# A fourth raw-weight buffer, one buffer fewer for a tanh, and q/k rows that are no longer loaded

## The chip, the cores and the metric

The kernel runs on one core of one Trainium2 chip. The metric is the device time of one execution in microseconds. The kernel before took 527.47 us, the median of three runs (524.8 to 528.14).

## What is computed

A gated linear attention is followed by two feed-forward layers. The reference walks through 768 positions of 16 (batch, head) pairs; the kernel computes the same in chunks of 128 positions.

```python
for t in range(S):
    m_new = np.maximum(f_gate[:, :, t] + m, i_gate[:, :, t])
    f_stab = np.exp(f_gate[:, :, t] + m - m_new)
    i_stab = np.exp(i_gate[:, :, t] - m_new)
    C = f_stab * C + i_stab * outer(vt, kt)
    n = f_stab * n + i_stab * kt
    y[:, :, t] = sigmoid(o_gate[t]) * (C @ qt) / max(abs(n . qt), 1)
# layer one: 1536 tokens x 320, hidden width 1536
xn = x / sqrt(mean(x * x) + 1e-6) * rms_g
x = (silu(xn @ w_gate) * (xn @ w_val)) @ w_out
# layer two
out = (sigmoid(x @ w_gate2) * (x @ w_val2)) @ w_out2
```

All inputs and the output are float32. The sizes are B, H, S, D = 2, 8, 768, 40.

## The kernel before

The work has three parts that overlap. The attention works on 12 units, one for each chunk of 128 positions and batch (`unit`, u = 0 to 11). A unit loads q and k in a layout of 104 partitions (`qk`: four heads on rows 0 to 39, four on rows 64 to 103, rows 40 to 63 zero), its natural rows `nat` and the transposed q `qt`, forms decay factors `E` with an exponential on ACT (L313 or L307), scores on PE (L323), weighs them on DVE (L330), and multiplies with v on PE (L343). The scores read rows 0 to 39 and 64 to 103 of `qk` alone (L322). Two units make one token group of 256 tokens.

Layer one runs over six token groups and 12 blocks of 128 hidden units (`up1`, `act1`, `dn1`): 16 matmuls of 256 columns into one PSUM bank `up` (L460), a tanh on ACT (L489), two products on DVE (L490, L491), a split of the result into two float32r parts (L492, L493), and six matmuls into the accumulators (L471 to L473). Layer two does the same with its own weights. Its token groups are of 256, 512, 512 and 256 tokens (`G2`). For groups of 512 the gate goes to a bank `up` and the value to a bank `sc`, the tanh (L544) writes a tile `th2` in SBUF, L545 multiplies in it, L546 and L547 read it.

The float32 weights are split into two float32r parts on the chip. A layer has 12 blocks, each in two pieces of 128 x 544 words, so 24 pieces a layer; here they are numbered 0 to 47, and block m of layer one has pieces 2m and 2m+1. A piece goes through these steps, each an instruction of 0.7 us or so:

- load (L98, issued by SyncE) into a buffer `wraw`, of which there are three
- L102 (`w_pre`, ACT) reads it and writes `wT`, of which there are also three
- L109 (`w_low`, ACT) rewrites the low half of `wraw` in place; it needs nothing but the landed words
- L113 (`w_bits`, DVE) joins both into `wT`; it is the last reader of `wraw`
- L122 (`w_hi`, ACT) writes the high part `wH`
- L126 (`w_lo`, DVE) writes the low part `wL`, and `wT` is free

The 24 pieces of layer one are made while the first token group goes through the layer, up to 96 us. The pieces of layer two are made from 238 us on, while groups 4 and 5 of layer one and group 0 of layer two take turns on PE, block by block, up to 341 us; a block's weights go where layer one's block of one before lay, so they follow its last use.

Each engine executes in order. Up to the first two units the order is written out; after that a scheduler sets it from priorities (`want` with times from the table `T`), from dependencies and from free buffers in its own model of time. SyncE issues nearly all loads, in order, so a load that waits for its buffer holds up the loads behind it.

Of the kernel before, what the change touches and what calls it, by code (L numbers as in the profile page):

```python
# [7 lines left out]
F32 = mybir.dt.float32  # L8
F32R = mybir.dt.float32r
BF16 = mybir.dt.bfloat16  # L10
I32 = mybir.dt.int32
# [6 lines left out]
B, H, S, D = 2, 8, 768, 40  # L18
# [17 lines left out]
WP = WC // 2  # L36
# [22 lines left out]
def attention_then_two_moe(tc, fi, fir, qk, qt3, nat, w1, w2, rms_g, consts, out):  # L59
    nc = tc.nc  # L60
# [5 lines left out]
    mp = ctx.enter_context(tc.tile_pool(name="mp", bufs=2))  # L66
# [27 lines left out]
    wH, wL, wraw, wT = {}, {}, {}, {}  # L94

    def w_load(moe, m, p):
        t = wraw[moe, m, p] = mp.tile([128, WP, 2], I32, tag="wraw", name="wraw", bufs=3)
        nc.sync.dma_start(out=t, in_=w64[moe][m, :, p * WP:(p + 1) * WP, :])  # L98

    def w_pre(moe, m, p):  # L100
# [141 lines left out]
    def a_load(u, parts=(0, 1, 2, 3)):  # L242
        d = X.setdefault(u, {})
        if 0 in parts:
            d["qk"] = ap.tile([QR, 2, 4, L], F32, tag="qk", name="qk")
            nc.sync.dma_start(out=d["qk"], in_=qk[u])
        if 1 in parts:
            d["nat"] = ap.tile([128, NAT], F32, tag="nat", name="nat")
            nc.sync.dma_start(out=d["nat"][:, 9 * D:], in_=nat[u, :, 9 * D:])
        if 3 in parts:  # L250
            nc.sync.dma_start(out=d["nat"][:, 0:9 * D], in_=nat[u, :, 0:9 * D])
        if u >= B and 2 in parts:
            d["qt"] = ap.tile([KR, NG, L], F32, tag="qt", name="qt")
            nc.sync.dma_start(out=d["qt"], in_=qt3[u])
# [254 lines left out]
    p2 = [None]  # L509
# [27 lines left out]
    def act2(g, m, gt, vl):  # L537
        if G2[g][1] == 2:
            th = mp.tile([128, 256], F32, tag="th", name="th")
            hT = hts[1, g, m] = mp.tile([128, 2, 256], F32R, tag="hT", name="hT", bufs=3)  # L540
        else:
            th = p2[0].tile([128, 512], F32, tag="th2", name="th2")
            hT = hts[1, g, m] = p2[0].tile([128, 2, 512], F32R, tag="hT2", name="hT2", bufs=3)
        nc.scalar.activation(th, gt, AF.Tanh, scale=0.5)  # L544
        nc.vector.scalar_tensor_tensor(out=th, in0=th, scalar=1.0, in1=vl, op0=ALU.add, op1=ALU.mult)  # L545
        nc.scalar.copy(hT[:, 0, :], th)  # L546
        nc.vector.tensor_tensor(out=hT[:, 1, :], in0=th, in1=hT[:, 0, :].bitcast(F32), op=ALU.subtract)  # L547
# [54 lines left out]
    def w_step(k):  # L602
        moe, m, p = piece(k)
        if k < 3:
            return
        t = t_slot(first(moe, None, m)) + T["w1" if moe else "w0"] + p
        if k > 3:
            want(t - T["wld"], lambda: w_load(moe, m, p))
        want(t - 3, lambda: w_pre(moe, m, p))
        want(t - 2, lambda: w_bits(moe, m, p))  # L610
        want(t - 1, lambda: w_hi(moe, m, p))
        want(t, lambda: w_lo(moe, m, p))

    def unit(u):
        t = t_unit(u) + (u % B) * T["skew"]
        st = [
            [a_scale, a_bcast_pe, a_exp] if u > B else [a_scale, a_exp],
            [a_scores, a_wv, a_gate],
            [a_weigh] if u < PE_ADD else [a_weigh, a_state],
            [a_out, a_decay, a_state, a_update] if u < PE_ADD else [a_out, a_decay, a_update],  # L620
            [a_norm1, a_norm1b, a_norm1c],
            [a_norm2],
            [a_norm3, a_flip],
            [a_xt],
        ]
        if u >= B:
            want(t - T["uld"], lambda: a_load(u))
        for k, fns in enumerate(st):
            want(t + k * T["stg"], *[lambda fn=fn: fn(u) for fn in fns])
# [7 lines left out]
    with tc.manual_schedule(engines=set(engines)):  # L637
        nc.vector.memset(junk, 0.0)
        nc.sync.dma_start(out=fi0, in_=fi[:, :, 0:L])
        nc.scalar.dma_start(out=fiS, in_=fi[:, :, L:])  # L640
        a_load(0, (0,))
        w_load(0, 0, 0)
        nc.scalar.copy(tiny, junk[:, 0:1])
        for t, fill in ((ident, 1.0), (identb, 1.0)):
# [33 lines left out]
        g_max()  # L678
        w_pre(0, 0, 0)
        w_load(0, 0, 1)  # L680
        a_load(1, (0,))
        a_load(0, (1,))
        g_move()
# [92 lines left out]
    for s, (moe, g, m, f, l) in enumerate(steps):  # L776
        if s == 0:
            att_ctx.close()
            p2[0] = ctx.enter_context(tc.tile_pool(name="p2", bufs=2))
        if s == NI:  # L780
            for k in range(2 * NM, 2 * NM + 2):
                w_step(k)
        r = []
        want(t_slot(s), lambda: in_order(lambda: r.append((up1, up2)[moe](g, m))))
        want(t_slot(s) + 1, lambda: (act1, act2)[moe](g, m, *r[0]))
        if s > 1:
            dn(s - 2)
            x2_ready(s - 2)
            if steps[s - 2][0:2] == (0, 5) and steps[s - 2][2] < NM - 1:
                for k in range(2):  # L790
                    w_step(2 * NM + 2 * (steps[s - 2][2] + 1) + k)
# [73 lines left out]
```

## Time and profile before

| | |
|---|---|
| median of three runs | 527.47 us |
| lowest, highest | 524.8, 528.14 us |
| the profiled execution, device time | 524.49 us |
| its span, first to last instruction | 522.7 us |
| PE busy | 503.7 us |
| DVE, ACT, POOL busy | 260.4, 232.0, 105.3 us |
| moved by DMA | 43.09 MB |

The profile is of one execution, and its rows are in microseconds from the start of its span. Busy PE means that a matmul is under way, not that PE is at its peak, since matmuls are pipelined. A row of the list of waits says which engine stood idle before which instruction, what ended the wait, and the total, the number of times and the longest.

### The profile page before, as it was taken

To read this page: it belongs to the slowest core of one execution; us is meant where nothing else is said; L and a number is where in the kernel's file an instruction comes from. 1 tells how busy PE (TensorE), PEld (TensorE's weight loads), DVE (VectorE), ACT (ScalarE), POOL (GpSimd) and SP (SyncE) were. 2 spreads that over 40 slices of the span, in tenths; PEclk is the share of its full clock that TensorE was granted. 3 is DMA by queue.
4 is the path that set the end of the run, shared out by engine and by line. 5 is a ranking of instruction groups with operands and counts; after the bars stand their busy time and mean duration, and the time that the engine had idled before them with its cause. 6 is when DMAs were issued, how large, how long until landed. Compare 5 with 4: busy or idle time off the path is not lost.

```text
span 522.7 us, 9043 instructions
## 1 busy us (share of the span) xinstructions
PE 503.7 (96%) x3576; PEld 466.8 (89%) x3576; DVE 260.4 (50%) x540; ACT 232.0 (44%) x518; POOL 105.3 (20%) x164
## 2 busy tenths in 40 slices
PE   7889899999999999999999899999999999999996
PEld 5668799999999999999999899998888888888996
DVE  5668789744255445557665646533233233222332
ACT  4667889733233333326576657442222222221322
POOL 7013135443243243232221211110000000000000
PEclk9769979999999999999999999999999999999999
DMA  6588787711041030102153242000000010000100
GB/s 193 182 255 298 246 262 231 240 55 41 1 112 44 25 114 16 41 2 85 35 198 113 92 165 87 1 1 25 1 1 2 0 51 0 1 0 1 51 1 26
DMA packets 15752, 43.09 MB, mean 82 GB/s; under 512 B 1822, under 2 KB 6734, under 8 KB 15710
## 3 DMA queue, kind: packets, MB, share of 16 engines
q1 hardware_dynamic: 15518, 42.27, 25.4%
q8 instruction: 28, 0.46, 0.4%
q10 hardware_dynamic: 192, 0.25, 0.1%
q14 instruction: 14, 0.11, 0.1%
HBM read 40.32 MB, written 2.01 MB: 81 GB/s over the span
## 4 chain that ended last, share of the span: by engine, by line
PE 76%; DMA 10%; ACT 6%; DVE 5%; issue 2%; SPq 0%; ACTq 0%; DVEq 0%
PE up L460 34%; DMA wraw<-in_w_dram 9%; PE sc L460 9%; PE dn L471 5%; PE dn L473 5%; PE dn L472 5%; PE at L343 4%; PE sc L323 2%; DVE wT L113 2%; PE at L471 2%; PE at L472 2%; PE at L473 2%; ACT wT L102 2%; ACT wH L122 2%; ACT wraw L109 1%
## 5 line engine op out<-in xcount | busy, mean ns | idle before, releaser
L460 PE MATMUL up<-xT,wH 128*128 128x256 f32 x940 | 165.4, 290 | 4.2 <-DVE th L491 4.0
L460 PEld LDWEIGHTS up<-xT,wH 128*128 128x128 f32 x940 | 136.0, 192 | 7.5 <-DVE th L491 5.4
L460 PE MATMUL up<-xT,wL 128*128 128x256 f32 x564 | 101.2, 287 | 0.3 <-DVE wL L126 0.3
L493 POOL TENSOR_TENSOR hT<-th,hT 128x256 fp32r<-128x256 f32 x72 | 57.7, 802 | 152.0 <-ACT hT L492 112.7
L460 PEld LDWEIGHTS up<-xT,wL 128*128 128x128 f32 x564 | 82.3, 192 | 0.7 <-DVE wL L126 0.5
L471 PE MATMUL dn<-wH,hT 128*128 128x320 f32 x184 | 58.1, 316 | 0.0
L490 DVE SCALAR_TENSOR_TENSOR th<-th,up 128x256 f32<-128x256 f32 x72 | 30.1, 418 | 56.2 <-ACT th L489 55.8
L472 PE MATMUL dn<-wL,hT 128*128 128x320 f32 x184 | 57.4, 313 | 0.0
L473 PE MATMUL dn<-wH,hT 128*128 128x320 f32 x184 | 56.9, 316 | 0.0
L544 ACT ACTIVATE th<-up 128x256 f32<-128x256 f32 (+1 forms) x48 | 23.4, 488 | 72.8 <-PE up L460 72.8
L545 DVE SCALAR_TENSOR_TENSOR th<-th,sc 128x512 f32<-128x512 f32 x24 | 16.5, 687 | 64.1 <-PE sc L460 63.9
L546 ACT CAST hT<-th 128x256 fp32r<-128x256 f32 (+1 forms) x48 | 24.6, 513 | 49.9 <-DVE th L545 49.8
L489 ACT ACTIVATE th<-up 128x256 f32<-128x256 f32 x72 | 27.3, 380 | 41.3 <-PE up L460 39.9
L109 ACT ACTIVATE wraw<-wraw 128x544 int32<-128x544 uint16 x48 | 34.0, 708 | 25.4 <-DMA wraw<-in_w_dram 25.0
L492 ACT CAST hT<-th 128x256 fp32r<-128x256 f32 x72 | 29.1, 404 | 34.6 <-DVE th L491 34.6
L113 DVE SCALAR_TENSOR_TENSOR wT<-wT,wraw 128x544 int32<-128x544 int32 x48 | 36.9, 772 | 12.8 <-ACT wT L102 7.7
L547 DVE TENSOR_TENSOR hT<-th,hT 128x256 fp32r<-128x256 f32 (+1 forms) x48 | 28.1, 585 | 25.0 <-ACT hT L546 24.9
L126 DVE TENSOR_TENSOR wL<-wT,wH 128x544 fp32r<-128x544 f32 x46 | 34.2, 770 | 7.1 <-ACT wH L122 6.9
L471 PEld LDWEIGHTS dn<-wH,hT 128*128 128x128 f32 x184 | 35.0, 190 | 1.2
L102 ACT ACTIVATE wT<-wraw 128x544 f32<-128x544 f32 x48 | 33.2, 702 | 6.2 <-DMA wraw<-in_w_dram 5.9
L472 PEld LDWEIGHTS dn<-wL,hT 128*128 128x128 f32 x184 | 34.9, 190 | 0.9
L473 PEld LDWEIGHTS dn<-wH,hT 128*128 128x128 f32 x184 | 34.3, 189 | 0.3 <-issue 0.2
(184 smaller groups left out, 821.5 us busy)
## 6 DMA issues: line engine op xcount, KB each, us to landing
wraw<-in_w_dram SPq DMA_DIRECT2D x48, 544.0 KB, 4.8
qk<-in_qk_dram SPq DMA_DIRECT2D x12, 416.0 KB
nat<-in_nat_dram SPq DMA_DIRECT2D x12, 324.0 KB, 2.8
nat<-in_nat_dram SPq DMA_DIRECT2D x12, 180.0 KB, 6.3
qt<-in_qt_dram SPq DMA_DIRECT2D x10, 180.0 KB, 2.8
out_dram<-x2n SPq DMA_DIRECT2D x11, 160.0 KB, 1.9
rows<-x2n SPq DMA_DIRECT2D x6, 30.0 KB
gB<-in_rms_g_dram SPq DMA_DIRECT2D x1, 160.0 KB
```

The lines of the kernel that those rows point to most:

```text
L102: nc.scalar.activation(t.bitcast(F32), wraw[moe, m, p][:, :, 1].bitcast(F32), AF.Prelu, scale=2.0 ** -112, alpha=2.0 ** 32)
L109: nc.scalar.activation(raw[:, :, 0], top, AF.Copy, scale=2.0 ** -13, bias=2.0 ** -14 - 0.5)
L113: nc.vector.scalar_tensor_tensor(out=t, in0=t, scalar=3, in1=raw[:, :, 0], op0=ALU.logical_shift_left, op1=ALU.bitwise_or)
L126: nc.vector.tensor_tensor(out=wL[moe, m][:, sl], in0=wT.pop((moe, m, p)).bitcast(F32), in1=wH[moe, m][:, sl].bitcast(F32), op=ALU.subtract)
L460: mm = nc.tensor.matmul(o, lhsT=a, rhs=b, start=(n == 0), stop=(n == 7))
L471: nc.tensor.matmul(o, lhsT=hi, rhs=wo[0], start=first, stop=False)
L472: nc.tensor.matmul(o, lhsT=hi, rhs=wo[1], start=False, stop=False)
L473: pe_last[0] = nc.tensor.matmul(o, lhsT=lo, rhs=wo[0], start=False, stop=last)
L490: nc.vector.scalar_tensor_tensor(out=th, in0=th, scalar=1.0, in1=gt, op0=ALU.add, op1=ALU.mult)
L492: nc.scalar.copy(hT[:, 0, :], th)
L493: nc.gpsimd.tensor_tensor(out=hT[:, 1, :], in0=th, in1=hT[:, 0, :].bitcast(F32), op=ALU.subtract)
L547: nc.vector.tensor_tensor(out=hT[:, 1, :], in0=th, in1=hT[:, 0, :].bitcast(F32), op=ALU.subtract)
```

## The change

The raw words get four buffers, the tile of layer two's tanh for 512 tokens gets one where it had two, and the load of q and k becomes two loads, of rows 0 to 39 and of rows 64 to 103; rows 40 to 63 of the buffer are left as they are.

```diff
-        t = wraw[moe, m, p] = mp.tile([128, WP, 2], I32, tag="wraw", name="wraw", bufs=3)
+        t = wraw[moe, m, p] = mp.tile([128, WP, 2], I32, tag="wraw", name="wraw", bufs=4)
...
-            nc.sync.dma_start(out=d["qk"], in_=qk[u])
+            for r in (0, 64):
+                nc.sync.dma_start(out=d["qk"][r:r + D], in_=qk[u, r:r + D])
...
-            th = p2[0].tile([128, 512], F32, tag="th2", name="th2")
+            th = p2[0].tile([128, 512], F32, tag="th2", name="th2", bufs=1)
```

Lines from 247 on stand one later in the changed kernel. The scheduler orders the instructions anew. Three places follow, each first before and then after.

On SyncE near 24 us, behind the six sends of `rows`; L98 loads raw words, L246 (L247 after) q and k, L254 (L255) the transposed q.

```order
L98 DMA wraw<-in_w_dram 128x1088
L246 DMA qk<-in_qk_dram 104x1024
L254 DMA qt<-in_qt_dram 120x384
L246 DMA qk<-in_qk_dram 104x1024
L254 DMA qt<-in_qt_dram 120x384
L98 DMA wraw<-in_w_dram 128x1088
```

```order
L98 DMA wraw<-in_w_dram 128x1088 x2
L247 DMA qk<-in_qk_dram 40x1024 x2
L255 DMA qt<-in_qt_dram 120x384
L247 DMA qk<-in_qk_dram 40x1024 x2
L255 DMA qt<-in_qt_dram 120x384
L98 DMA wraw<-in_w_dram 128x1088
```

The load of piece 5 has moved ahead of the loads of units 2 and 3; the last row was that of piece 5 and is that of piece 6.

On ACT near 58 to 63 us, where PE's scores of unit 4 wait for the exponential L307 (L308 after). The rows before begin with L102 and L109 of piece 13.

```order
L102 ACTIVATE wT<-wraw 128x544
L109 ACTIVATE wraw<-wraw 128x544
L489 ACTIVATE th<-up 128x256
L109 ACTIVATE wraw<-wraw 128x544
L122 CAST wH_1283<-wT 128x544
L391 ACTIVATE rd<-at 128x8
L102 ACTIVATE wT<-wraw 128x544
L307 ACTIVATE E<-sc 128x512
```

After, the rows begin with L102 of piece 12.

```order
L102 ACTIVATE wT<-wraw 128x544
L109 ACTIVATE wraw<-wraw 128x544
L392 ACTIVATE rd<-at 128x8
L109 ACTIVATE wraw<-wraw 128x544
L102 ACTIVATE wT<-wraw 128x544
L490 ACTIVATE th<-up 128x256
L109 ACTIVATE wraw<-wraw 128x544
L102 ACTIVATE wT<-wraw 128x544
L122 CAST wH_1295<-wT 128x544
L308 ACTIVATE E<-sc 128x512
```

The L109 rows are those of pieces 13 and 14 before, and of pieces 13, 14 and 15 after; L102 of piece 14 and L122 of piece 12 stand just ahead of the exponential in both.

On ACT near 321 to 325 us, at the end of layer two's opening, with the last two L109 of the kernel (pieces 46 and 47).

```order
L109 ACTIVATE wraw<-wraw 128x544
L489 ACTIVATE th<-up 128x256
L122 CAST wH_3836<-wT 128x544 x2
L109 ACTIVATE wraw<-wraw 128x544
L492 CAST hT<-th 128x256
L102 ACTIVATE wT<-wraw 128x544
```

```order
L109 ACTIVATE wraw<-wraw 128x544
L490 ACTIVATE th<-up 128x256
L122 CAST wH_3848<-wT 128x544 x2
L493 CAST hT<-th 128x256
L102 ACTIVATE wT<-wraw 128x544
```

The first row is that of piece 46 before and of piece 47 after. From the opening's end on, this missing L109 is the only difference in ACT's sequence but for a few neighbours that change places before 104 us; one L109 more stands before 104 us.

## Rows read from the trace of the kernel before

**Rows 1.** The page: PE's busy time; clock granted and DMA share in 40 slices.

```profile
PE 503.7 (96%) x3576; PEld 466.8 (89%) x3576; DVE 260.4 (50%) x540; ACT 232.0 (44%) x518; POOL 105.3 (20%) x164
...
PEclk9769979999999999999999999999999999999999
DMA  6588787711041030102153242000000010000100
```

**Rows 2.** List of waits: engine line waited for: us, times, longest.

```profile
ACT wraw L109 <- DMA wraw<-in_w_dram: 25.0, 24, 2.1
...
PEld up L460 <- DVE th L491: 5.4, 8, 1.4
```

**Rows 3.** The waits of SyncE's queue, same columns.

```profile
SPq L98 <- DVE wT L113: 27.1, 18, 4.5
```

**Rows 4.** The chain that ended last: start, us, what.

```profile
54.67 0.74 DVE wT L113
55.42 6.17 DMA wraw<-in_w_dram
61.62 0.69 ACT wraw L109
64.03 1.15 PE sc L323 x8
...
264.98 3.70 DMA wraw<-in_w_dram
...
317.72 3.75 DMA wraw<-in_w_dram
```

**Rows 5.** Timeline of ACT, then of PE, 61 to 64.1 us.

```profile
61.62 0.69 ACT L109 ACTIVATE wraw<-wraw 128x544 int32<-128x544 uint16 x1 [1.22 <-DMA wraw<-in_w_dram]
63.40 0.58 ACT L307 ACTIVATE E<-sc 128x512 f32<-128x512 f32 x1
...
64.03 0.37 PE L323 MATMUL sc<-qk 40*128 40x128 f32 x1 [2.06 <-ACT E L307]
```

**Rows 6.** Waits of PE's weight loads, 279 to 328 us, and the timeline's last.

```profile
PEld up L460 <- DVE th L491: 4.9, 6, 1.4
...
327.29 0.53 PEld L460 LDWEIGHTS up<-xT,wH 128*128 128x128 f32 x4 [0.86 <-DVE th L491]
```

**Rows 7.** Windows: stretch, us, busy times; last columns: clock, DMA share, GB/s.

```profile
26.00:34.00 8.00, 5.80 (x31) 3.92 (x29) 5.54 (x17) 3.32 (x9) 1.09 (x2) 0.71 0.92 251
36.00:51.40 15.40, 15.40 (x124) 14.06 (x122) 11.84 (x20) 12.61 (x26) 4.31 (x5) 0.90 0.93 314
51.40:53.10 1.70, 1.70 (x16) 1.50 (x15) 1.59 (x4) 1.70 (x5) 0.00 (x0) 1.00 0.08 33
...
66.31:73.14 6.83, 6.83 (x30) 6.17 (x29) 6.33 (x13) 5.26 (x13) 1.89 (x3) 0.50 0.77 232
```

**Rows 8.** Timeline of ACT, 321 to 325 us.

```profile
323.49 0.72 ACT L109 ACTIVATE wraw<-wraw 128x544 int32<-128x544 uint16 x1
324.10 0.39 ACT L492 CAST hT<-th 128x256 fp32r<-128x256 f32 x1
```

**Rows 9.** Timeline of DVE and ACT, 354 to 357 us.

```profile
354.98 0.69 DVE L547 TENSOR_TENSOR hT<-th,hT 128x512 fp32r<-128x512 f32 x1 [0.69 <-ACT hT L546]
...
356.29 0.60 ACT L544 ACTIVATE th<-up 128x512 f32<-128x512 f32 x1 [1.34 <-PE up L460]
```

**Rows 10.** DMA packets: a 104-row load, two of 128 rows, one of 40.

```profile
DMA packets 117, 0.43 MB, mean 122 GB/s; under 512 B 13, under 2 KB 13, under 8 KB 117
...
DMA packets 288, 1.11 MB, mean 124 GB/s; under 512 B 32, under 2 KB 32, under 8 KB 288
...
DMA packets 50, 0.03 MB, mean 44 GB/s; under 512 B 10, under 2 KB 50, under 8 KB 50
```

**Rows 11.** Timelines of SyncE from 0 us and of ACT near 9 us.

```profile
2.46 0.90 SPq L98 DMA_DIRECT2D wraw<-in_w_dram  x2
...
9.19 2.17 ACT L313 ACTIVATE E<-up,early 128x128 f32<-128x128 f32 x8 [0.57 <-DVE early L224]
```

## The prediction

> **What bounds the kernel now.** I read the page first. TensorE is busy for 96% of the span, but the slices of its granted clock and of the DMA engines say that the first fifth is another regime: there the clock is not always granted in full and the DMA engines are nearly full [rows 1]. The list of waits comes next. ACT waits 25.0 us in 24 places at L109 for raw weight words to land, and PE's weight loads wait 5.4 us in 8 places for DVE's L491 [rows 2]. The queue view of SyncE names the other end: 18 loads of raw words waited for a DVE L113, 27.1 us in all [rows 3]. L113 is the last reader of a raw buffer, so with three buffers the load of piece k is held until the L113 of piece k-3.
>
> The chain that ended last shows that this loop matters twice [rows 4]. At 54.67 an L113 ends, a load is issued at 55.42, ACT's L109 takes it up at 61.62 and PE's scores follow at 64.03. From 264.98 to 317.72, where layer two's words are made while layer one is finished, seven loads of raw words stand in the chain.
>
> What it costs PE is read from PE's own gaps. At 61.97 it stops for 2.06 us: ACT's exponential at 63.40, which frees the bank, stands behind an L109 that idled 1.22 us for its words [rows 5]. In layer two's opening PE's weight loads idle six times for L491, 4.9 us in all, the last time 0.86 us [rows 6]. Everything after 330 us is PE without gaps.
>
> **The fourth raw buffer.** Read alone it lets every load go one piece earlier: piece k waits for L113 of k-4. That would be worth the gaps just added, 2.1 + 4.9 = 7.0 us. The order of the instructions says otherwise. L109 needs no result but the landed words, and the scheduler uses the new buffer to put it one piece further ahead on ACT. In the opening the L109 of piece 14 stood ahead of L122 and the exponential; now that of piece 15 stands there. Piece 14's load waited for the L113 of piece 11; piece 15's load, with four buffers, waits for the L113 of piece 11 too. ACT stops at the same place for a load that the same event releases. In layer two's opening ACT's sequence is the same row by row until its last L109, and one L109 was moved in before 104 us, so each L109 there handles the next piece and its load again waits for the same L113. I therefore put both gaps down as unchanged.
>
> What is left are the two ends of the loop. At the start one load, that of piece 5, goes out behind piece 4 near 24.2 us instead of at 31.23, past four loads of attention data in SyncE's queue. It gains nothing in a stretch whose DMA engines are full: 0.92 from 26 to 34 us at 251 GB/s and 0.93 from 36 to 51.4 us at 314 GB/s [rows 7]. The extra piece, 544 KB or 557,056 bytes, takes 557,056 / 314,000 = 1.8 us of transfer there (2.2 us at the slower rate), and what follows lands later by up to that. DMA first runs empty from 51.4 to 53.1 us, share 0.08, which is just long enough to take it back [rows 7]. So I take 0 for the opening, between -2.1 us (the gap at 61.97 goes) and +1.8 us (the displacement reaches the chain).
>
> At the end of layer two's opening there is one L109 fewer to do. It is the one at 323.49, which starts 0.61 us before the cast at 324.10 that waits behind it [rows 8]; the L102, L113 and L491 behind that cast move up with it, and the last of the six gaps, 0.86 us, ends 0.6 us earlier. I take -0.6 us, between -0.9 and 0.
>
> **One buffer for layer two's tanh.** A tanh must now wait until L547 of the step before has read the old one. The tightest pair of the 23 is the first but one: L547 starts at 354.98, takes 0.69 us and ends at 355.68 by the finer clock, and the next tanh starts at 356.29 because PE is only then done [rows 9]. That leaves 0.61 us; most later pairs leave 1.0 to 1.7 us. The wait is covered by PE's own work, 0. Nothing can be gained from a buffer less. If the cover were gone, only the two pairs with 0.6 us would be late, by tenths of a microsecond, and PE would write the gate of the next step into a second bank meanwhile: 0 to +0.3 us.
>
> **The q and k rows.** Twelve loads of 416 KB become 24 of 160 KB, 96 KB (98,304 bytes) less a unit. By bytes, at 314 GB/s, a load is shorter by 0.31 us; the six of units 2 to 7 lie in full stretches, so by bytes this is -1.9 us. The DMA view speaks against that [rows 10]. A load of 104 rows shows 117 packets, 13 of them small; two loads of 128 rows show 32 small ones, 16 each; a transfer of 40 rows shows 50 packets, 10 of them small. If there is one small packet for each DMA engine that takes part, 104 rows go 8 to an engine over 13 engines, and 40 rows go 4 to an engine over 10. Two such transfers, if they use the same engines, put 8 rows on each of them again, and what the busiest engine carries is unchanged. I take 0, with -1.9 us as one end.
>
> The Trainium skill, "DMA: Bandwidth & Descriptors", section "Why a DMA increments its semaphore by 16 and not by 1", states this as a rule: a transfer uses the largest number of engines up to 16 that divides its rows, the lowest-numbered ones. By it 104 gives 13 and 40 gives 10, which the packets above agree with; without it the sum would be 1.9 us lower. That the engines are the lowest-numbered ones no row here shows.
>
> The other end is SyncE's issue. An issue takes it about 0.33 us, and four instead of two q and k loads stand in its first 5 us. The first raw words then come some 0.4 us later; ACT idles 0.57 us after them, before 9.19, which covers it [rows 11]. 0, up to +0.3 us.
>
> **Sum.** 0 (opening) - 0.6 (last L109) + 0 (tanh) + 0 (rows) = -0.6 us. On the profiled execution, 524.49 us, this gives 523.9. The median of the three runs, 527.47, is 2.98 us above the profiled execution, so the forecast for a median is 526.9 us. The forecast's own range takes the smaller uncertainties: 523.5 to 530.
>
> **Rivals.**
> The buffer leads by a whole piece after all: ACT no longer idles at L109, and both sets of gaps go, 527.47 - 7.0 = 520.5. For it speaks that 18 loads were issued as soon as a buffer came free; against it the order, in which L109 moved on by the same one piece. The Trainium skill, "Perfetto Trace Analysis", section "Optimization Strategy", says that a gap that repeats on the engine that should be full can mean too little SBUF for the next tile, which is this rival; the six gaps agree with its description, and the order decides whether one more tile is enough.
>
> The rows are worth their bytes: -1.9 - 0.6 = -2.5, 525.0. For it speaks DMA's share of 0.93, against it the small packets.
>
> The slower side: the displaced 1.8 us reaches the L109 ahead of the exponential at 63.40. PE's gap there grows from 2.06 to 3.9 us. From 66.31 to 73.14, after that gap, the granted clock is 0.50 [rows 7], the lower of the two levels (1.2 of 2.4 GHz). A longer gap could bring half as much again of this, 3.4 us at half the clock, 1.7 us of work lost. Sum 1.8 + 1.7 - 0.6 = +2.9, 530.4. It decides once DMA, with one more piece ahead, is not done by 53.1 us. For it speaks the full DMA from 26 us on, against it the 1.7 us in which DMA ran empty.
>
> **How the numbers follow.** The forecast has 0.60, the whole lead 0.12, the bytes 0.12, the displaced load 0.16. A measurement of this kernel tells about 1% from no change, 5.3 us: faster is below 522.2, slower above 532.7. Faster takes most of the whole lead, 0.11, and 0.04 from the forecast and the bytes, where the lower clock after 66 us could also vanish (3.4 us): 0.15. Slower takes a third of the displaced load, where the lower clock lasts longer still, and 0.01 of the rest: 0.06. Within 1% is 0.79. The range leaves out the far part of the first rival and the worst of the last: 521.8 to 530.8.
>
> **What would show it.** Right: SyncE's loads of raw words still wait for L113, ACT's L109 still idles at the same places in both stretches, near 61.6 and at 284 to 322 us, with the six gaps within 0.3 us of theirs but the last; no tanh L544 of 512 columns waits for L547; 20 small packets for a unit's q and k. Wrong: gaps from 280 to 328 us that sum to less than 2.5 us (the whole lead), shorter waits for words only near q and k loads (the bytes), or a gap near 62 us above 3 us and a longer stretch of lower clock behind it (the displaced load).

## The result, and the profile after

The changed kernel took 520.44 us (median of 4 runs, 517.26 to 522.97) beside 526.13 us for the kernel before (4 runs): ratio 0.9885, 95% interval 0.9838 to 0.9931. Timed once more in 12 runs beside 33 of before (e13 below) it took 520.45 us beside 524.87: 0.9935, interval 0.9899 to 0.9970. So the change gains near 1%, 3 to 6 us; the forecast was 0.6 us. The three runs of before that the forecast started from (median 527.47) were also high: the medians of before in the four later comparisons, 108 runs, are 523.9 to 525.0. Some runs fall in a slower state; ratios leave these out, and the profiles of e15 and e16, taken in it, are left out of the comparisons of stretches below.

The profiled execution of after took 520.55 us, its span is 518.8 us. The page, the parts of [rows 1]:

```profile
PE 502.5 (97%) x3576; PEld 465.4 (90%) x3576; DVE 259.5 (50%) x540; ACT 231.7 (45%) x518; POOL 104.5 (20%) x164
...
PEclk9859999999999999999999999999999999999999
DMA  5589777521031020102063341000000010000100
```

In [rows 1] the clock row has a 7 in the sixth slice; here it is 9. Windows of after (stretch, us, busy time of PE, PEld, DVE, ACT and POOL, granted clock, DMA share, GB/s), against [rows 7]:

```profile
60.00:66.00 6.00, 4.95 (x36) 4.43 (x36) 5.04 (x10) 5.42 (x12) 2.77 (x4) 1.00 0.87 298
66.31:73.14 6.83, 5.89 (x48) 5.21 (x49) 6.83 (x15) 6.35 (x14) 2.64 (x4) 1.00 0.77 251
23.30:37.00 13.70, 12.10 (x53) 9.03 (x52) 9.64 (x27) 6.30 (x15) 1.83 (x3) 0.50 0.71 228
```

The 6.83 us at half clock behind the gap at 62 us are gone: PE has 48 matmuls in that stretch, not 30. The only long stretch at 0.50 is the one from 23.3 us, where PE has 53 matmuls in 13.7 us.

The list of waits of after, as [rows 2], and SyncE's row, as [rows 3]:

```profile
ACT wraw L109 <- DMA wraw<-in_w_dram: 24.1, 23, 3.9
...
PEld up L461 <- DVE th L492: 4.4, 8, 1.4
```

```profile
SPq L98 <- DVE wT L113: 17.7, 11, 4.8
```

ACT waits for raw words nearly as long as before (25.0 us in 24 places), and PE's weight loads wait for the same instruction (L492 is L491 of before; from line 247 on, lines stand one further down). SyncE's loads still wait for L113, in 11 places where it was 18. A fourth buffer has been added, and the wait that it was to remove is there.

The place near 62 us, as [rows 5]; ACT, then PE:

```profile
60.85 0.70 ACT L109 ACTIVATE wraw<-wraw 128x544 int32<-128x544 uint16 x1 [0.58 <-DMA wraw<-in_w_dram]
...
62.57 0.59 ACT L308 ACTIVATE E<-sc 128x512 f32<-128x512 f32 x1
```

```profile
63.21 1.16 PE L324 MATMUL sc<-qk 40*128 40x128 f32 x8 [1.03 <-ACT E L308]
```

The L109 ahead of the exponential idles 0.58 us, not 1.22, and PE's gap is 1.03 us, not 2.06.

Layer two's opening, as [rows 6], 276 to 325 us:

```profile
PEld up L461 <- DVE th L492: 3.6, 5, 1.4
```

Five gaps with 3.6 us, where there were six with 4.9.

To see where the 3.9 us of span went, I mark time by PE's up steps (a group of 16 matmuls at L460, 120 in all), counted from 0:

| stretch | before | after | e13 (after again) |
|---|---|---|---|
| start to up step 0 | 34.00 | 34.36 | 32.64 |
| step 0 to 24 (opening) | 106.77 | 104.81 | 104.98 |
| step 24 to 54 | 120.04 | 119.92 | 119.95 |
| step 54 to 80 (layer two's opening) | 77.73 | 76.30 | 75.82 |
| step 80 to 119 | 175.20 | 175.20 | 175.20 |
| step 119 to the end | 9.00 | 8.24 | 8.23 |

So 2.0 us come from the opening, 1.4 from layer two's opening and 0.8 from the last nine microseconds, and the start gives 0.4 back. These are single profiles. The profile of e3 below, which has before's order on every engine and before's loads, shows 104.6 us for step 0 to 24, so one profile does not show that the 2.0 us are the change's.

The tail can be read off at once. The last output's issue, by ACT's timeline of before and of after:

```profile
519.11 0.36 ACTq L562 DMA_DIRECT2D out_dram<-x2n  x1
```

```profile
515.95 0.36 ACTq L563 DMA_DIRECT2D out_dram<-x2n  x1
```

That is 3.63 us ahead of the span's end in before and 2.87 us in after. The DMA view of before from 519.2 us and that of after from 516 us:

```profile
DMA packets 289, 0.34 MB, mean 96 GB/s; under 512 B 32, under 2 KB 288, under 8 KB 288
...
q14 instruction: 1, 0.01, 0.6%
```

```profile
DMA packets 288, 0.33 MB, mean 117 GB/s; under 512 B 32, under 2 KB 288, under 8 KB 288
```

In before one packet of instructions is fetched there, beside the 288 of the outputs; in after none.

### The profile page after: what moved, and what is told of

It reads as the page before. It is cut to its first block, busy times and chain, and to the rows that moved or that the text cites. A ratio compares the mean times of both kernels' runs of the same rounds, so it can differ in the third digit from the quotient of the medians.

```text
span 518.8 us, 9056 instructions
## 1 busy us (share of the span) xinstructions
PE 502.5 (97%) x3576; PEld 465.4 (90%) x3576; DVE 259.5 (50%) x540; ACT 231.7 (45%) x518; POOL 104.5 (20%) x164
## 3 DMA queue, kind: packets, MB, share of 16 engines
q1 hardware_dynamic: 15314, 41.09, 24.1%
## 4 chain that ended last, share of the span: by engine, by line
PE 69%; DMA 14%; DVE 7%; ACT 6%; issue 3%; POOL 0%; SPq 0%; ACTq 0%; DVEq 0%; POOLq 0%
PE up L461 31%; DMA wraw<-in_w_dram 13%; PE sc L461 9%; PE dn L472 5%; PE dn L474 5%; PE dn L473 4%; PE at L344 3%; ACT wT L102 2%; DVE wT L113 2%; ACT wraw L109 2%; PE sc L324 2%; PE at L473 2%; PE at L472 2%; PE at L474 2%; DVE wL L126 1%
## 5 line engine op out<-in xcount | busy, mean ns | idle before, releaser
L461 PE MATMUL up<-xT,wH 128*128 128x256 f32 x940 | 163.3, 287 | 2.6 <-DVE th L492 2.6
L461 PEld LDWEIGHTS up<-xT,wH 128*128 128x128 f32 x940 | 134.3, 190 | 5.3 <-DVE th L492 4.4
L461 PE MATMUL up<-xT,wL 128*128 128x256 f32 x564 | 99.4, 284 | 0.9 <-DVE wL L126 0.9
L461 PEld LDWEIGHTS up<-xT,wL 128*128 128x128 f32 x564 | 81.0, 189 | 1.2 <-DVE wL L126 1.1
L491 DVE SCALAR_TENSOR_TENSOR th<-th,up 128x256 f32<-128x256 f32 x72 | 30.1, 418 | 55.5 <-ACT th L490 55.0
L545 ACT ACTIVATE th<-up 128x256 f32<-128x256 f32 (+1 forms) x48 | 23.5, 490 | 71.9 <-PE up L461 71.9
L109 ACT ACTIVATE wraw<-wraw 128x544 int32<-128x544 uint16 x48 | 33.9, 708 | 24.3 <-DMA wraw<-in_w_dram 24.1
L113 DVE SCALAR_TENSOR_TENSOR wT<-wT,wraw 128x544 int32<-128x544 int32 x48 | 36.3, 762 | 14.0 <-ACT wT L102 10.0
L102 ACT ACTIVATE wT<-wraw 128x544 f32<-128x544 f32 x48 | 33.2, 701 | 6.8 <-DMA wraw<-in_w_dram 6.5
```

Of the source, the lines that this page charges most:

```text
L102: nc.scalar.activation(t.bitcast(F32), wraw[moe, m, p][:, :, 1].bitcast(F32), AF.Prelu, scale=2.0 ** -112, alpha=2.0 ** 32)
L109: nc.scalar.activation(raw[:, :, 0], top, AF.Copy, scale=2.0 ** -13, bias=2.0 ** -14 - 0.5)
L113: nc.vector.scalar_tensor_tensor(out=t, in0=t, scalar=3, in1=raw[:, :, 0], op0=ALU.logical_shift_left, op1=ALU.bitwise_or)
L461: mm = nc.tensor.matmul(o, lhsT=a, rhs=b, start=(n == 0), stop=(n == 7))
```

## The experiments

Two theories stood after the first comparison. By the first, the time follows the order of instructions that the scheduler picks, and each edit matters by the order that it brings. By the second, the edits themselves act on the transfers. The first four runs take the parts alone, in whatever order the scheduler gives them.

**The parts alone.** e1 keeps the two `bufs` edits and loads q and k whole; e2 has only the two q and k loads; e3 only `bufs=1` for `th2`. (Four raw buffers with two for `th2` were not run.) e4 is the changed kernel with each scheduled L109 issued behind the L102 of its own piece, in both layers:

```diff
-        nc.scalar.activation(t.bitcast(F32), ..., AF.Prelu, ...)
-        w_low(moe, m, p)
+        pre = nc.scalar.activation(t.bitcast(F32), ..., AF.Prelu, ...)
+        with tc.issue_after(pre.ins) if moe or 2 * m + p > 2 else ExitStack():
+            w_low(moe, m, p)
```

> Four raw buffers and one tanh buffer, q and k loaded whole as before. If the fourth buffer earned the gain: 520 to 522 us. If the rows left out earned it: 525 to 527 us, like before. If it was the order that the scheduler happened on together with a stretch of lower clock: anything from 520 to 527, and the granted clock near 65 to 73 us tells which.

> Only the split load of q and k. If the rows earned it by their bytes: 521 to 523 us, with ACT's waits at L109 before 96 us shorter by 1.5 us or more in total. If the buffer earned it: 525 to 527 us with the same waits as before; the first raw words land later, since two more issues stand ahead of them.

> Only the tanh buffer. Every engine's order is the same as before, so all theories expect 526 us, within 0.5%; it shows the scatter of a kernel that differs in nothing else, and a tanh of 512 columns that waits for L547 would show as a gap on PE after 350 us of which I expect none.

> The changed kernel with each L109 held behind the L102 of its own piece, so that no piece's L109 runs ahead on ACT. If L109 run ahead is what makes ACT stop for loads, the fourth buffer now leads by a whole piece: ACT's waits for raw words in 278 to 322 us fall from some 12 us to under 3 us, PE's gaps there go, and the time is 515 to 517 us. If the gaps come from the order of wT and the block's reuse instead: 520 us like the changed kernel, with the gaps of 0.4 to 1.3 us still there.

Measured: e1 1.0029 (0.9993 to 1.0065), e2 1.0173 (1.0115 to 1.0230), e3 1.0010 (0.9978 to 1.0043), e4 0.9894 (0.9836 to 0.9951). The tanh buffer costs nothing. The other parts do not add: nothing and +1.7% alone, a gain together. No expectation had e2's time. e4's median, 518.3 us, lies above the 515 to 517 expected, though its waits for raw words and PE's gaps in layer two's opening are gone as expected. In e2 the chain that ended last shows one place of the loss:

```profile
91.85 5.81 DMA wraw<-in_w_dram
...
97.69 0.68 ACT wraw L109
98.37 0.29 ACT hT L493
98.66 0.38 ACT xT L431
...
99.09 0.51 PE up L461 x2
```

and PE's timeline the price, with the windows behind it:

```profile
99.09 0.51 PE L461 MATMUL up<-xT,wH 128*128 128x256 f32 x2 [2.64 <-ACT xT L431]
```

```profile
101.70:105.10 3.40, 3.40 (x18) 3.40 (x18) 0.62 (x3) 2.21 (x5) 0.24 (x1) 0.50 0.16 48
```

ACT's L431, which PE needs for the next up step, stands behind an L109 that waits for words. PE idles 2.64 us and then has half its clock for 3.4 us. Nothing of this names the q and k loads.

A second loss stands just ahead of layer two's opening, at 247 to 261 us. In e1, e2 and e11 (below) PE idles 1.9 to 2.3 us there for DVE's `x2T`, layer two's input; no other profile has more than 0.6 us, and step 24 to 54 takes 124.3 to 125.4 us where before takes 120.0. In e1, whose opening is the shortest of all (102.2 us from step 0 to 24), this stretch takes 5.1 us back, with 3.4 us at half clock behind the gap:

```profile
249.41 0.39 PE L471 MATMUL sc<-wH,hT 128*128 128x320 f32 x1 [2.01 <-DVE x2T L432]
```

**One edit, one order.** To part an edit from its order I held the order: every instruction that the scheduler may move gets an order-only dependency (it adds no wait) on the one that stood ahead of it on its engine in another build, `seq` being that build's order:

```diff
+        for a, b in zip(seq, seq[1:]):
+            tc.add_manual_dep(mine[b], mine[a].name, NO_SYNC, reason="pin")
```

e5 is the split alone in before's order; e6 four buffers and whole loads in the changed kernel's order; e7 the changed kernel in before's order; e8 the kernel before with PE, DVE and POOL in the changed kernel's order (its ACT and SyncE cannot follow with three buffers). The traces show e5, e7, e9 and e10 in before's order on every engine.

> The split q and k loads alone, with every engine's instructions held in the order of the kernel before by added order-only dependencies (no waits are added; SyncE has the second half of each load right behind the first). Theory A (the time follows the order that the scheduler picks, the rows themselves are worth nothing): within 0.5% of before, ratio 0.995 to 1.005, and none of the +1.7% that the split alone showed with its own order. Theory B (the loads themselves do it: two issues, 20 small packets, fewer bytes): the +1.7% stays, ratio 1.012 to 1.022. By bytes alone (1.9 us): ratio 0.996.

> Four raw buffers and one tanh buffer with whole q and k loads, held in the changed kernel's order on every engine. Theory A (order): the changed kernel's gain is there without its q and k edit, ratio 0.984 to 0.993, and no half-clock stretch near 66 us. Theory B (loads): no gain, ratio 0.998 to 1.007 as with the same code in its own order (1.003).

> The changed kernel (four raw buffers, one tanh buffer, split loads) held in the order of the kernel before. Theory A in its plain form (order alone): as before, ratio 0.996 to 1.004. Rival, the lead of a whole piece: with L109 kept where it was on ACT, each load is released one L113 earlier, ACT no longer waits at L109 in layer two's opening, the six gaps of PE there (4.9 us) and the one at 62 us (2.1 us) go: ratio 0.984 to 0.991. The sum of both parts of the prediction (L109 moving on takes the lead away) holds if this one gains and the scheduler's own order of four buffers alone (1.003) does not.

> The kernel before (three raw buffers, two tanh buffers, whole loads) with TensorE, VectorE and GpSimd held in the changed kernel's order; ACT and SyncE follow in an order of their own, since three buffers cannot keep the changed kernel's place of L109. Theory A (the order of PE, DVE and POOL in the opening is what gains): ratio 0.985 to 0.995, about 1.7 us or more of PE's lead at 115 us. Rival (the fourth buffer is needed, by loads that land earlier or by L109's place): ratio 0.998 to 1.01.

e9 adds the missing cell, e10 splits the load with all its bytes (52 and 52 rows), e11 is the kernel before in e2's order.

> Four raw buffers and one tanh buffer with whole q and k loads, held in the order of the kernel before on every engine; the cell that is missing beside before (1), the split alone in that order (0.994) and both in that order (0.989). If the two edits add: ratio 0.990 to 0.998, with 4 to 5 us of PE's lead gained from 280 to 328 us, since L109 keeps its place there. If the buffer only pays once the q and k loads are smaller: 0.998 to 1.004.

> The q and k rows in two loads of 52 rows, all 104 rows, so the bytes of before with the two issues of the change; order of the kernel before on every engine. If the split's -0.64% comes from the bytes that are not moved: ratio 0.997 to 1.003. If it comes from two smaller transfers that share the engines differently: ratio 0.991 to 0.996, as with the rows left out.

> The kernel before, held in the order that the scheduler picked for the split alone (e2, ratio 1.017). If that order is what cost it, and the split itself gains 0.6%: ratio 1.015 to 1.03, with 6 us or more of PE's lead lost between 88 and 110 us. If the split loads were to blame: 0.997 to 1.003.

| run | raw buffers | q and k loads | order | ratio, 95% interval | step 54 to 80, us |
|---|---|---|---|---|---|
| before | 3 | whole | before's | 1 | 77.73 |
| e5 | 3 | split | before's | 0.9936 (0.9909 to 0.9964) | 76.10 |
| e10 | 3 | halves, all bytes | before's | 0.9950 (0.9912 to 0.9987) | 74.98 |
| e9 | 4 | whole | before's | 0.9892 (0.9860 to 0.9925) | 72.47 |
| e7 | 4 | split | before's | 0.9885 (0.9835 to 0.9934) | 72.47 |
| e8 | 3 | whole | after's (PE, DVE, POOL) | 0.9997 (0.9962 to 1.0033) | 76.43 |
| e16 | 3 | split | after's (PE, DVE, POOL) | 0.9951 (0.9914 to 0.9988) | – |
| e6 | 4 | whole | after's | 0.9940 (0.9905 to 0.9976) | 76.22 |
| after, e13 | 4 | split | after's | 0.9885, 0.9935 | 76.30, 75.82 |
| e1 | 4 | whole | its own | 1.0029 (0.9993 to 1.0065) | 76.27 |
| e11 | 3 | whole | e2's | 1.0175 (1.0113 to 1.0236) | 76.69 |
| e2 | 3 | split | e2's | 1.0173 (1.0115 to 1.0230) | 76.31 |

What follows. e11 has e2's time without e2's edit: the +1.7% is the order's alone. In e11 the same instruction, L430 before the line shift, holds PE up:

```profile
101.73 0.51 PE L460 MATMUL up<-xT,wH 128*128 128x256 f32 x2 [3.51 <-ACT xT L430]
```

```profile
103.20:110.00 6.80, 6.80 (x32) 6.80 (x32) 1.92 (x6) 3.27 (x8) 2.05 (x3) 0.50 0.17 53
```

So the first theory holds for e2. It does not carry the change: the changed kernel's order of PE, DVE and POOL is worth nothing in itself (e8; its order of ACT can't be had with three buffers), while each of the two edits alone gains 0.5 to 0.6% in it (e6, with ACT's order too, and e16). The ratios of e5 and e6 lie in the ranges of neither theory, that of e9 just below the range for edits that add. e1 and e2 hid what their edits gain under bad orders of their own. And the split gains with all bytes moved, too (e10); that the bytes add a part of 1.9 us, 0.4%, to e5's gain the two intervals don't exclude.

The buffer's own price stands in the last column. With every engine in the order of the kernel before, L109 included, four buffers make step 54 to 80 5.3 us shorter, and PE does not idle at all. Windows of before, after, e9 and e1, each from its step 54 to its step 80; the second number is the length, the third PE's busy time:

```profile
260.81:338.54 77.73, 74.34 (x574) 72.50 (x573) 45.87 (x88) 48.29 (x104) 14.91 (x18) 1.00 0.33 113
```

```profile
259.09:335.39 76.30, 73.92 (x575) 72.45 (x573) 46.18 (x88) 47.84 (x103) 15.18 (x18) 1.00 0.33 108
```

```profile
261.33:333.80 72.47, 72.47 (x575) 72.47 (x574) 45.68 (x88) 48.80 (x104) 14.67 (x18) 1.00 0.34 115
```

```profile
260.54:336.81 76.27, 73.74 (x574) 72.45 (x573) 46.13 (x88) 47.73 (x103) 15.31 (x18) 1.00 0.33 109
```

In e9 the list of ACT's waits has no row for L109 in this stretch; in before it has 16.4 us, in after 14.7, in e1 15.1. Each length here is from one profile. The other profiles in which L109 idles (e2, e3, e5, e8, e10 and e11 with three buffers, e1, e6 and e13 with four) lie between 75.0 and 76.8 us; so the 1.4 us by which after is under before are not shown to be the buffer's.

**L109 held, with four buffers and with three.** e12 is the changed kernel with e4's edit in layer two alone (`if moe`). e14 is e12 with three raw and two tanh buffers, PE, DVE and POOL in e12's order; e15 is e12 with whole loads, all engines in e12's order. e13 is the changed kernel again, e16 is e8 with the split.

> The changed kernel with each L109 of layer two issued behind its own L102, so that it no longer runs ahead there; the opening is left to the scheduler. If the lead of the fourth buffer is free to be had in layer two's opening: PE gains about 4 us more there than the changed kernel does, its gaps from 280 to 328 us go to under 1 us in all, ratio 0.978 to 0.986. If what is gained there is lost again elsewhere (granted clock): 0.986 to 0.992.

> The changed kernel once more, unchanged, for the size of its gain. Theory (both edits gain about 0.6% each in the opening, nothing in layer two's opening): ratio 0.986 to 0.992, and 275 to 278 us from PE's up step 54 to step 80 of 120 less one another's start, that is no shorter than with three buffers. Rival (most of the first measurement was chance): 0.993 to 1.0.

> e12 with three raw buffers and two tanh buffers again: L109 of layer two behind its own L102, split loads, TensorE, VectorE and GpSimd in e12's order, ACT and SyncE in their own. If the fourth buffer is what empties PE's gaps from 280 to 328 us: the gaps stay at 1 to 3 us and the ratio is 0.990 to 1.0. If L109's place alone does it: no gaps there, 0.982 to 0.988.

> e12 with whole q and k loads, every engine in e12's order. If the split is worth its 0.5 to 0.6% beside four buffers too: ratio 0.989 to 0.994. If four buffers take up what the split gives (as e9 and e7 hint, 0.9892 and 0.9885): 0.983 to 0.989.

> The split loads with three raw buffers and two tanh buffers, TensorE, VectorE and GpSimd in the changed kernel's order (e8 with the split). If the split gains with three buffers whatever the order: ratio 0.990 to 0.996. If its gain in e5 belonged to that order: 0.997 to 1.003.

(In the text for e13 the length of the stretch is a slip: what it means is step 54 to 80, 76 to 78 us with three buffers.)

Measured: e12 515.70 us, 0.9855 (0.9802 to 0.9908); e13 0.9935, which lies in the range set for chance in the first measurement, not in that of the theory; e14 0.9945 (0.9907 to 0.9983); e15 0.9858 (0.9822 to 0.9895); e16 0.9951. Windows of e12 and of e14, step 54 to 80:

```profile
258.08:330.54 72.46, 72.46 (x574) 72.46 (x573) 46.01 (x88) 49.22 (x105) 15.78 (x18) 1.00 0.37 116
```

```profile
264.61:337.07 72.46, 72.46 (x574) 72.46 (x573) 46.01 (x88) 49.20 (x105) 15.76 (x18) 1.00 0.40 123
```

e14 has no gaps: with L109 behind its own L102, three buffers are enough in layer two's opening. Its time does not follow. The ratio is that expected with the gaps, and no better than that of e16, which has them; so most of what is saved here seems to be lost elsewhere. In e14's one profile step 24 begins at 144.8 us (before 140.8, e12 138.2); why is open.

In layer two's opening, what counts is the number of buffers less the pieces by which L109 runs ahead on ACT. From layer two's fifth piece on, L109 stands mostly one to two pieces ahead of its own L102 in before, two to three in after; it stands behind it in e12 and e14. Three buffers with one to two and four with two to three leave gaps; four with one to two (e7, e9) and three with none (e14) leave no gap; nor does e4, four with none (72.47 us). (Holding L109 also moved a few other instructions: 52 of PE's 3576 places and 27 of DVE's 540 differ between after and e12.) e12 is faster than before by 1.5%; its median is 4.7 us below that of after, but their intervals overlap. e15 and e6, with whole loads and with and without L109 held, lie apart beyond their intervals (0.9858 and 0.9940). e15 beside e12 shows no gain of the split beside four buffers so held.

## Why the prediction was wrong

**The fourth buffer in layer two's opening: right.** The prediction said that L109 moves one piece further ahead, so that "ACT stops at the same place for a load that the same event releases". The traces show it: from piece 31 on each load is issued 0.03 us after the end of an L113, that of three pieces earlier in before and of four pieces earlier in after. The wait of 25.0 us is 24.1, the gaps of 4.9 us are 3.6, and the four profiles with four buffers and the run-ahead (after, e13, e1, e6) need as long for the stretch as those with three. e9 shows the other half of the argument: with the run-ahead taken away, the same buffer gains 5.3 us there. The term of -0.6 us for the last L109 can't be told from the scatter of that stretch.

**The rival of the whole lead** forecast 520.5 us, the time that came. It isn't what happened: its gaps are still there. It describes e9, where it priced the two places at 7.0 us and layer two's opening alone gave 5.3. A time that matches doesn't settle a mechanism.

**The opening: this step failed.** "So I take 0 for the opening" measured -2.0 us in the profile, -1.6 with the start. The timed runs speak for a gain there by subtraction alone: of 3.4 us (e13) to 6.0 (the first comparison), 0.8 are the tail's and at most 1.4 or so layer two's opening's, and the other stretches did not change; this leaves an estimated 1 to 4 us, and at the low end of e13's interval nothing. The opening is also where the displaced load was to cost time, and PE's gap at 62 us did not grow to 3 us.

What the argument missed there is seen at that gap. The same event did release the load: piece 15's is issued at 55.19 us, 0.03 us after L113 of piece 11, as piece 14's was at 55.42 in before. But L109 could start 5.66 us later, not 6.20; it idled 0.58 us, and the gap became 1.03 us shorter. The 6.83 us at half clock behind it, 3.4 us of work, are gone; new gaps (0.94 us at 71.9, 0.70 at 97.9) give a part back. The prediction put the gap down as unchanged by the argument of layer two although the order differs here on every engine. The total of L109's waits is nearly unchanged, but in these traces an L109 costs PE something where an exponential or a copy for PE stands right behind it, as e2 shows at its worst. And the prediction let the stretch at half clock vanish in a few cases only, though it is the larger sum.

Whether the change brought this is not shown. In e3, with before's order and loads, the gap is 0.73 us and the stretch at half clock, of 3.41 us, comes later, at 90.9 us. From step 0 to 24, five profiles with no stretch at half clock that begins between 40 and 130 us (after, e13, e1, e9, e12) needed 102.2 to 105.0 us, seven with 3.41 us of it (e3 among them) 104.1 to 106.9, and two with 6.83 us (before, e7) 106.8 and 107.9; e2 and e11, with the bad order, needed 109.3 and 112.0. By the timed runs the gain needs an edit (e6, e16, not e8). That it goes through these stretches is argued from single profiles, not shown, and the cause of the opening's gain stays open.

**The q and k rows: the 0 failed with three buffers.** A unit's two loads show 20 small packets. The DMA view around one unit's loads, in before and in after:

```profile
DMA packets 117, 0.43 MB, mean 185 GB/s; under 512 B 13, under 2 KB 13, under 8 KB 117
...
q1 hardware_dynamic: 117, 0.43, 57.7%
```

```profile
DMA packets 100, 0.33 MB, mean 164 GB/s; under 512 B 20, under 2 KB 20, under 8 KB 100
...
q1 hardware_dynamic: 100, 0.33, 51.0%
```

The windows are 2.3 and 2.0 us long. The packets took 0.577 x 2.3 x 16 = 21.2 us, over 13 engines 1.63 us each, and 0.51 x 2.0 x 16 = 16.3 us, over 10 engines 1.63 us each. If the small packets count the engines, and both loads of after use the same ten, each engine carried the same, as the prediction argued; another unit gave 2.1 us in before and 1.6 in after, so it is no exact rule. But with three buffers the split gains 0.5 to 0.6% in either order, in one of them with all bytes as well. Of those 3 us 0.8 are the tail; why two loads help the rest is open. Beside four buffers I found no such gain (e7 against e9, e15 against e12).

**The tail: not in the prediction.** 0.76 us of the change came after the last up step, a part that the sum did not have. In the profiles of before, e1, e3, e8 and e9 that part takes 8.98 to 9.01 us, in the others 8.14 to 8.24; the last section says what differs there.

**The tanh buffer: right.** e3 is 1.001 (the tightest pair that the prediction names is the first of the 23, not the second), and in after ACT's tanh waits from 320 us on only for PE (71.9 us in 41 places), never for DVE.

**The base.** Three runs set the base at 527.47; 108 more put it near 524.6. Of the 6.5 us between 526.9 and 520.4, 2.9 us were in the base and 0.8 in the tail; the rest is mostly the opening's.

## What to carry to other kernels

One more buffer is a lead only if the instruction that takes up the data keeps its place: see in the order whether the scheduler spends the buffer on running ahead, and if so hold the consumer back, which in layer two's opening closed PE's gaps with three buffers as with four. In the whole time it showed beside four buffers (e12, e15), not beside three (e14). An edit that lets a scheduler start over changes two things at once, and here the order alone was worth up to 2.4%; pin the order of one build on the other before an edit is praised or blamed. Take a base from as many runs as its scatter wants.

## What the runs showed of the hardware

A fetch of instructions can delay the landing of a program's last output. In before the DMA engines fetch 8 KB of instructions from 1.56 to 1.87 us after the last output's issue, and the output's last packet, of 4 bytes, ends with it, at 1.87 us; in after there is no fetch, and its last packet ends at 1.52. A load or store here tells of its landing by 16 counts of a semaphore. In before 15 of them have come by 1.93 us and the last at 2.72, and SyncE's closing wait for it ends at 2.73; in after all 16 have come by 1.86.

All 18 profiles agree. In before, e1, e3, e8 and e9 a fetch begins at 1.47 to 1.57 us, the last count comes at 2.71 to 2.74, and the end is long. In e6, e11 and e15 the fetch begins at 2.46 or 2.47 us, behind the last count, and in the other ten there is none; all these have the short end. It is not the added loads as such: e6, e11 and e15 load q and k whole. What sets the place of the fetch was not tried.

The granted clock's half stretches are not a property of the program alone. The changed kernel had one of 13.65 us from 23.3 us in one profile, and stretches of 3.41 us from 23.9 and 6.83 us from 30.8 us in another. PE's first up step began between 32.6 and 38.0 us in the profiles of all kernels. For a change of 1%, where these stretches fall is as large as what is measured, and a difference in one of them is no evidence for an edit until runs by the dozen agree.
